# Third batch's second quad: its roots moved amid the GELUs of the second w_in stage, with two more bank pairs for tiles 6 to 9

## The chip, the core and the metric

The kernel runs on one core of a Trainium2 chip. The metric is device time in microseconds (us) of one execution; lower is better. All times below are us unless marked ns. Engines are named as in the profile: PE (matrix multiply), ACT (activations), DVE (vector), POOL, and SP, which only issues DMAs.

## What is computed

Cosine attention over 8 batches, 12 heads, 448 positions and head size 64, followed by a feed-forward block with an exact GELU:

```python
q_n = q / (norm(q) + 1e-6);  k_n = k / (norm(k) + 1e-6)
scores = q_n @ k_n.T / tau
attn = softmax(scores)                 # over the keys
x = (attn @ v), heads joined           # 3584 x 768
out = gelu(x @ w_in) @ w_out           # 768 -> 2048 -> 768
```

Inputs and output are float32; the multiplications take bf16.

## The kernel before

**Work and stages.** Four heads make a *quad* (three to a batch); quads are counted through all batches, so quads 3, 4, 5 belong to the second batch (`b = 1`) and quads 6, 7, 8 to the third. For `b = 0` a stage `attention_first` runs, for the others `attention(b, fill)`; each is followed by `first(b)`, the w_in stage with its GELUs. The output product (w_out, `second_pieces`, line 352) of one batch is cut into single matmuls, `fill`, and these are run in portions (`run()`, line 597) between the attention steps of the next batch. The order of all instructions is written out by hand (`manual_schedule`): each engine executes its own queue in the order in which the program calls for it.

**Preparing a quad.** For each quad: load q and k (`load_qk`, SP, four buffers); square them on POOL (`square`, line 156); add the squares up on DVE (`reduce`, line 165, 2.0 us); take the root as exp(0.5 ln) on ACT (`logs` line 172, `roots` line 181); add 1e-6 on POOL (line 190) and take the reciprocal on DVE (line 192), both in `inverses`; multiply on POOL (`scale`, line 208, two instructions); and transpose by a DMA from SP (`transposes`, line 220). Roots are taken for a *group* of quads at once. These lists use *units*: unit u is quad u - 1, since quad 0 is cut in two. `groups` (line 114) holds lists of units: before, units 7 and 8 (quads 6 and 7) share group 6; units 9 and 10 share group 7. `upto(f, n)` calls f for all items below n that were not called yet, so a call with a small n can do nothing.

**Attention.** A quad has seven chunks of keys. `visit(b, pairs)` takes the next chunks of batch b: for each, scores (PE, line 246) into a pair of PSUM banks, and the exp (ACT, line 253) out of it. There are three pairs, `st0`, `st1` and `st2`. `both(g, p)` finishes quad g: sums of the exps (PE, line 275), `turned` and `inverted` and `spread` on DVE, values (PE, line 289) into bank pair p, and `normalise` (DVE, line 323), which writes x. Sums, output tiles and most tiles of the w_in stage use two more banks in turn, `mm0` and `mm1` (`mm_tile`); a finished output tile is copied out by DVE (line 356) and stored by SP.

**The w_in stage.** `first(b)` makes 16 tiles of 128 columns of x @ w_in, six matmuls each (line 655), and a GELU for each on ACT (line 691). `pairs` (line 650) says which tiles take a pair of banks: `{2: 0, 4: 1}` puts tiles 2 and 3 into `st0`, and 4 and 5 into `st1`; other tiles take `mm0` and `mm1` in turn. The first six tiles are begun with four of their six matmuls, and finished when x is complete. Ln and Exp use another activation table than Gelu, so ACT loads a table when it changes over (lines 647, 693, 695, 700). In batch 0 such a change stands behind tile 5's GELU already: `root(5)` is taken there. In all batches, `first(b)` prepares quads of the next batches: scale and transposes of two quads, a load, squares and sums of two quads.

Of the kernel before, what the change touches and what calls it, by code (L numbers as in the profile page):

```python
# [16 lines left out]
def kernel(  # L17
# [20 lines left out]
    NQ = H // 4  # L38
# [60 lines left out]
    def mm_tile(name, shape=(128, 512), dtype=F32, aside=None):  # L99
        t = ps_mm.tile(list(shape), dtype, tag=f"mm{turn[0] if aside is None else turn[0] ^ aside}", name=name)  # L100
        if aside is None:
            turn[0] ^= 1
        return t

    def pair(i, name):
        pool = third[0] if i == 2 else ps_st
        return pool.tile([128, 2, 512], F32, tag=f"st{i}", name=name)
# [3 lines left out]

    units = [(0, 0, 1), (0, 1, 2)] + [(g, 0, 2) for g in range(1, NG)]
    NU = len(units)
    groups = [[n] for n in range(NQ + 2)] + [[NQ + 2, NQ + 3], [2 * NQ + 1, 2 * NQ + 2]]
    for n in range(3 * NQ, NU, NQ):
        groups += [[n, n + 1], [n + 2]] if n + 2 < NU else [[n]]
    shapes = [[len(gr), 2, units[gr[0]][2] - units[gr[0]][1], C] for gr in groups]
# [51 lines left out]
    def logs(n):  # L169
        nq = nq_t.pop(n)  # L170
        ln_t[n] = nrm.tile(list(nq.shape), F32, tag="lq", name=f"lq{n}")
        nc.scalar.activation(ln_t[n], nq, AF.Ln, bias=tiny)

    def roots(n):
        ln = ln_t.pop(n)
        if n <= NQ:
            sr_t[n] = root2[n % len(root2)][:, :math.prod(shapes[n])]
            nc.scalar.activation(sr_t[n][:, :, 0], ln.rearrange("p j i s c -> p (j i s c)"), AF.Exp, scale=0.5)
        else:
            sr_t[n] = nrm.tile(list(ln.shape), F32, tag="sr", name=f"sr{n}")  # L180
            nc.scalar.activation(sr_t[n], ln, AF.Exp, scale=0.5)  # L181

    def inverses(n):
        sr = sr_t.pop(n)
        shape = [128] + shapes[n]
        se = nrm.tile(shape, F32, tag="se", name=f"se{n}")
        if n <= NQ:
            nc.vector.tensor_reduce(se.rearrange("p j i s c -> p (j i s c)"), sr, mybir.AxisListType.X, ALU.add)
        else:
            nc.gpsimd.tensor_scalar(se, sr, 1e-6, None, ALU.add)  # L190
        rn = nrm.tile(shape, F32, tag="rn", name=f"rn{n}")
        nc.vector.reciprocal(rn, se)  # L192
        rn_t[n] = rn
# [20 lines left out]
    def transposes(u, i=None):  # L214
        g, s0, s1 = units[u]
        qkb = qkb_t[g]
        if g not in qkT_t:
            qkT_t[g] = qkTp.tile([128, 2, C, 128], BF16, tag="qkT", name=f"qkT{g}")
        if i is None:
            nc.sync.dma_start_transpose(out=qkT_t[g].rearrange("p i c s -> p (i c) s"),  # L220
                                        in_=qkb.rearrange("p i c s d -> p (i c s d)"))
            return
        tp = tp_t[u, i] = mm_tile(f"tp{u}_{i}", (128, C, 128), BF16)
        for c in range(C):
            nc.tensor.transpose(tp[64 * s0:64 * s1, c, :], qkb[:, i, c, s0:s1].rearrange("p s d -> p (s d)"), ident)  # L225

    def copies(u, i):
        g, s0, s1 = units[u]
        rows = slice(64 * s0, 64 * s1)
        nc.vector.tensor_copy(qkT_t[g][rows, i], tp_t.pop((u, i))[rows])  # L230
# [94 lines left out]
    def both(g, p):  # L325
        sums(g)
        turned(g)
        inverted(g)
        spread(g, 0)
        spread(g, 1)  # L330
        values(g, p=p)
        normalise(g, 0)
        normalise(g, 1)
# [64 lines left out]
    def upto(f, n, last=None):  # L398
        last = {load_qk: NG, load_v: NV, root: len(groups), load_wi: 4, load_wo: 4}.get(f, NU)
        while done.get(f, 0) < min(n, last):  # L400
            done[f] = done.get(f, 0) + 1
            f(done[f] - 1)
# [180 lines left out]
    def visit(b, pairs):  # L583
        for p in pairs:
            n, c = passes[at.get(b, 0)]
            at[b] = at.get(b, 0) + 1
            scores(b * NQ + n, ((0, c), (1, c)), p)
            exps(b * NQ + n, ((0, c), (1, c)))

    def attention(b, fill):  # L590
        fill = list(fill)
        if len(fill) == 128:
            parts = iter((20, 18, 20, 22, 32, 16))
        else:
            parts = iter((20, 13, 14, 17, 16, 16) if b == 1 else (16, 14, 16, 18, 16, 16))

        def run():
            for _ in range(next(parts)):
                fill.pop(0)()

        x_t[b] = xp.tile([128, KD, S], BF16, tag="x", name=f"x{b}")
        g0, u = b * NQ, b * NQ + 1
        run()
        upto(scale, u + 3)
        upto(transposes, u + 3)
        if b == 1:
            upto(load_qk, g0 + NQ + 2)
            upto(square, u + 4)
        visit(b, (0, 1, 2))
        if b > 1:  # L610
            upto(scale, u + 4)
            upto(transposes, u + 4)
        run()
        visit(b, (0, 1, 2))
        run()
        upto(load_qk, g0 + NQ + 3)
        visit(b, (0, 1) if b <= 2 else (0, 1, 2))
        upto(reduce, u + 4)
        upto(square, u + 5)
        run()  # L620
        visit(b, (0, 1, 2))
        both(g0, 0)
        upto(load_v, b + 3)
        upto(load_qk, g0 + NQ + 4)
        visit(b, (1, 2))
        upto(reduce, u + 5)
        run()
        visit(b, (1, 2, 0))
        both(g0 + 1, 1)
        visit(b, (2, 0))  # L630
        n = 2 * b + 4
        if n < len(groups):
            logs(n)
            roots(n)
        run()
        both(g0 + 2, 2)
        if n < len(groups):
            inverses(n)
            done[root] = n + 1
            if b > 1:  # L640
                visit(b + 1, (0, 1))

    def first(b):
        sb, hf = divmod(b, 2)
        if hf == 0:
            g_t[sb] = gp.tile([128, KF, 2 * S], BF16, tag="g", name=f"g{sb}")
        nc.scalar.preload_act_table_set(GELU_SET)
        u = (b + 1) * NQ + 1
        hps = {}
        pairs = {2: 0, 4: 1} if b else {0: 1, 2: 0, 6: 1, 8: 0}  # L650
        ahead = 6 if b else 5

        def mm(m, kds):
            for kd in kds:
                nc.tensor.matmul(hps[m], lhsT=wi[:, kd, m * 128:(m + 1) * 128],  # L655
                                 rhs=x_t[b][:, kd, :], start=(kd == 0), stop=(kd == KD - 1))

        def bank(m):
            if m in pairs:
                st = pair(pairs[m], f"hp{b}_{m}")  # L660
                hps[m], hps[m + 1] = st[:, 0, :S], st[:, 1, :S]
            elif m not in hps:
                hps[m] = mm_tile(f"hp{b}_{m}")[:, :S]

        for m in range(ahead):
            bank(m)
            mm(m, range(KD - 2))
        if b == 0:
            upto(square, u + 3)
            upto(scale, u + 1)  # L670
            upto(transposes, u + 1)
            upto(load_wo, 4)
            upto(reduce, u + 3)
        else:
            upto(scale, u + 2)
            upto(transposes, u + 2)
            upto(load_qk, (b + 1) * NQ + 5)
            upto(square, u + 4)
            upto(reduce, u + 4)
        for m in range(ahead):  # L680
            mm(m, range(KD - 2, KD))
        for m in range(KF):
            if b == 0 and m == 8:
                for i in range(2):
                    transposes(4, i)
                    copies(4, i)
            if m >= ahead and (m == 0 or m - 1 not in pairs):
                for k in range(m, m + 1 + (m in pairs)):
                    bank(k)
                    mm(k, range(KD))  # L690
            nc.scalar.activation(g_t[sb][:, m, hf * S:(hf + 1) * S], hps.pop(m), AF.Gelu)  # L691
            if b == 0 and m == 5:
                nc.scalar.preload_act_table_set(EXP_SET)
                upto(root, 6)
                nc.scalar.preload_act_table_set(GELU_SET)
                upto(scale, u + 2)
                upto(transposes, u + 2)
                upto(load_qk, 2 * NQ + 1)
        if b + 1 < B:
            nc.scalar.preload_act_table_set(EXP_SET)  # L700
            if b <= 1:
                visit(b + 1, (0, 1, 2))
            upto(root, 2 * b + 6)

    upto(load_qk, 1)
    nc.scalar.preload_act_table_set(EXP_SET)
# [3 lines left out]
    late = nrm.tile([128, 1], F32, tag="late", name="late", bufs=1)  # L710
# [56 lines left out]
```

## Time and profile before

| | us |
|---|---|
| median of 8 runs | 415.7 (415.43 to 417.17) |
| profiled execution, its own time | 415.43 |
| its span, first to last instruction | 413.7 |
| stage `attention(1)` on PE | 53.0 to 80.5 |
| stage `first(1)` on PE | 80.5 to 98.8 |
| stage `attention(2)` on PE | 99.5 to 132.2 |

All times in the text are from the start of the span. A group line of the profile reads: line, engine, operation, output<-input, shapes, count; then busy time and the mean in ns of one; then the idle time of the engine before them and what ended it. Timelines give start and duration. PE's matmuls are pipelined and their ends are modelled: where one follows another at pace, its modelled end lies behind the other's start. The largest groups:

```profile
L253 ACT ACTIVATE pt<-st 128x896 bf16<-128x896 f32 x168 | 142.9, 916 | 66.6 <-PE st L246 66.3
L352 PE MATMUL op<-wo,g 128*128 128x384 bf16 x864 | 147.8, 326 | 0.0
L655 PE MATMUL hp<-x,wi 128*128 128x448 bf16 x768 | 146.8, 353 | 0.0
L691 ACT ACTIVATE g<-hp 128x448 bf16<-128x448 f32 x128 | 65.9, 545 | 70.7 <-PE hp L655 70.5
L208 POOL TENSOR_TENSOR qkb<-qk,rn 128x896 bf16<-128x896 f32 (+1 forms) x49 | 79.6, 1651 | 40.6 <-DVE rn L192 40.6
L165 DVE TENSOR_REDUCE nq<-sq 128x28 f32<-128x1792 f32 (+2 forms) x30 | 48.8, 1637 | 57.6 <-POOL sq L156 54.8
```

### The profile page before, as it was taken

What the parts mean: (1) busy time and instruction counts of PE and PEld (TensorE: products, weight loads), DVE (VectorE), ACT (ScalarE), POOL (GpSimd) and SP (SyncE); (2) the same over time, 40 slices, a digit from 0 to 9 for tenths busy, and PEclk for the clock granted to TensorE, in tenths of its full rate; (3) what the DMA queues carried; (4) which work ended last, traced back from release to release, by engine and by line L of the source; (5) the groups of instructions that cost most, each with busy time, mean ns of one, the idle gap of its engine ahead of it and who ended that gap; (6) DMA issues with size and microseconds to landing.
All of it is one profiled execution on the core that took longest, in us unless ns stands there. A gap on an engine that the chain in (4) does not pass through costs nothing.

```text
span 413.7 us, 8268 instructions
## 1 busy us (share of the span) xinstructions
PE 407.1 (98%) x3506; PEld 212.5 (51%) x3506; DVE 188.4 (46%) x379; ACT 246.3 (60%) x358; POOL 167.0 (40%) x113
## 2 busy tenths in 40 slices
PE   7999999999999999999999999999999999999996
PEld 3444554555555555555555555555555555555564
DVE  4777217913278222943148331783118711481021
ACT  6895686546646567654764658755665467754300
POOL 4999706083810919054730537217370233000000
PEclk9999999999999999999999999999999999999999
DMA  8999998734396505935296332965078120510033
GB/s 289 259 261 207 205 232 279 177 68 112 64 224 200 124 11 91 287 87 122 21 222 207 68 105 46 217 189 133 2 143 218 40 44 2 120 41 0 0 78 77
DMA packets 66996, 54.53 MB, mean 132 GB/s; under 512 B 38672, under 2 KB 62352, under 8 KB 66960
## 3 DMA queue, kind: packets, MB, share of 16 engines
q1 hardware_dynamic: 54464, 41.79, 39.2%
q0 software_dynamic: 12112, 11.80, 18.0%
q8 instruction: 27, 0.44, 0.4%
q10 hardware_dynamic: 384, 0.43, 0.3%
q14 instruction: 9, 0.07, 0.1%
HBM read 45.61 MB, written 11.01 MB: 137 GB/s over the span
## 4 chain that ended last, share of the span: by engine, by line
PE 94%; DMA 2%; ACT 1%; DVE 1%; POOL 1%; issue 0%; SPq 0%; POOLq 0%
PE hp L655 35%; PE op L352 32%; PE st L246 9%; PE o L289 8%; PE sm L275 4%; PE spin L407 2%; DMA qk<-in_k_dram 2%; PE op L371 1%; PE sm L266 1%; PE tp L225 1%; ACT pt L253 1%; POOL sq L156 1%; DVE nq L165 0%; DVE qkT L230 0%; ACT g L691 0%
## 5 line engine op out<-in xcount | busy, mean ns | idle before, releaser
L253 ACT ACTIVATE pt<-st 128x896 bf16<-128x896 f32 x168 | 142.9, 916 | 66.6 <-PE st L246 66.3
L352 PE MATMUL op<-wo,g 128*128 128x384 bf16 x864 | 147.8, 326 | 0.0
L655 PE MATMUL hp<-x,wi 128*128 128x448 bf16 x768 | 146.8, 353 | 0.0
L352 PEld LDWEIGHTS <-g 128*128 128x128 bf16 x864 | 81.5, 98 | 62.3 <-issue 10.9
L655 PEld LDWEIGHTS <-wi 128*128 128x128 bf16 x768 | 74.4, 98 | 71.4 <-issue 2.9
L691 ACT ACTIVATE g<-hp 128x448 bf16<-128x448 f32 x128 | 65.9, 545 | 70.7 <-PE hp L655 70.5
L208 POOL TENSOR_TENSOR qkb<-qk,rn 128x896 bf16<-128x896 f32 (+1 forms) x49 | 79.6, 1651 | 40.6 <-DVE rn L192 40.6
L165 DVE TENSOR_REDUCE nq<-sq 128x28 f32<-128x1792 f32 (+2 forms) x30 | 48.8, 1637 | 57.6 <-POOL sq L156 54.8
L356 DVE COPY ot<-op 128x384 f32<-128x384 f32 x54 | 29.5, 548 | 95.5 <-PE op L352 93.4
L156 POOL TENSOR_TENSOR sq<-qk 128x1792 f32<-128x1792 f32 (+1 forms) x22 | 66.5, 3037 | 12.8 <-DMA qk<-in_k_dram 12.8
L190 POOL TENSOR_SCALAR se<-sr 128x28 f32<-128x28 f32 (+1 forms) x14 | 4.4, 312 | 125.4 <-ACT sr L181 125.3
L246 PE MATMUL st<-qkT 64*64 64x448 bf16 x672 | 47.7, 358 | 0.2
L289 PE MATMUL o<-pt,v 64*64 64x448 bf16 x672 | 36.9, 352 | 0.0
L246 PEld LDWEIGHTS <-qkT 64*64 64x64 bf16 x672 | 18.3, 105 | 23.8 <-issue 15.4
L318 DVE STREAM_TRANSPOSE rs<-rc 128x448 f32<-128x448 f32 x48 | 28.1, 623 | 0.8
L323 DVE TENSOR_TENSOR x<-o,rs 128x448 bf16<-128x448 f32 x48 | 27.0, 599 | 1.0 <-DVE rs L318 0.5
L192 DVE RECIPROCAL rn<-se 128x28 f32<-128x28 f32 (+2 forms) x18 | 6.8, 376 | 43.4 <-POOL se L190 43.2
L289 PEld LDWEIGHTS <-v 64*64 64x64 bf16 x672 | 17.7, 106 | 16.9 <-issue 8.4
L297 DVE STREAM_TRANSPOSE tr<-sm 128x448 f32<-128x448 f32 x24 | 15.5, 647 | 13.8 <-PE sm L275 10.7
L275 PE MATMUL sm<-pt,ones 128*32 128x448 bf16 (+1 forms) x336 | 17.8, 332 | 0.3 <-DVE ot L356 0.3
L309 DVE TENSOR_REDUCE tr<-tr 32x28 f32<-32x28 f32 x84 | 16.4, 196 | 1.6
L407 PE MATMUL spin<-blank,ident 128*128 128x448 bf16 x34 | 10.5, 458 | 2.2 <-DVE root L89 1.9
(43 smaller groups left out, 115.8 us busy)
## 6 DMA issues: line engine op xcount, KB each, us to landing
qk<-in_q_dram SPq DMA_DIRECT2D x23, 448.0 KB, 6.6
qk<-in_k_dram SPq DMA_DIRECT2D x23, 448.0 KB, 8.6
out_dram<-ot SPq DMA_DIRECT2D x48, 192.0 KB, 3.4
v<-in_v_dram POOLq DMA_DIRECT2D x7, 672.0 KB, 11.7
wi<-in_moe_w_in_dram POOLq DMA_DIRECT2D x8, 384.0 KB, 13.1
wo<-in_moe_w_out_dram POOLq DMA_DIRECT2D x4, 768.0 KB, 13.3
out_dram<-ot SPq DMA_DIRECT2D x12, 96.0 KB, 2.2
qk<-in_q_dram SPq DMA_DIRECT2D x2, 224.0 KB, 3.5
```

Of the source, the lines that this page charges most:

```text
L156: eng.tensor_tensor(sq[:, part], t[:, part], t[:, part], ALU.mult)
L165: nc.vector.tensor_reduce(nq[:, part], sq[:, part], mybir.AxisListType.X, ALU.add)
L208: eng.tensor_tensor(qkb[:, i, :, s0:s1].rearrange("p c s d -> p s c d"), t[:, i, s0:s1], rn[:, i].to_broadcast([128, s1 - s0, C, D]), ALU. ...
L246: nc.tensor.matmul(st[cols, n, :S], lhsT=qkT[rows, 1, c, cols], rhs=qkT[rows, 0, :, cols], start=True, stop=True, tile_position=(64 * s, 6 ...
L253: nc.scalar.activation(pt[:, :m], st[:, :m, :S], AF.Exp, scale=inv_tau)
L275: nc.tensor.matmul(bank_t[g, "sm"][r:r + 32, cols], lhsT=ones, rhs=pt_t[g, s, c][:, cols], start=(c < 2), stop=(c >= C - 2), tile_position ...
L289: nc.tensor.matmul(bank_t[g, h][cols, :S], lhsT=v_t[g][rows, s, c, :], rhs=pt_t[g, s, c][rows], start=(c == 0), stop=(c == C - 1), tile_po ...
L318: nc.vector.transpose(rs, bank_t[g, "rc"][:, h].to_broadcast([128, NB, 32]))
L352: nc.tensor.matmul(ps[:, :NH], lhsT=g_t[sb][:, kf, t * 128:(t + 1) * 128], rhs=wo[:, kf, ni * NH:(ni + 1) * NH], start=(kf == 0), stop=(kf ...
L356: nc.vector.tensor_copy(ot[:, ni * NH:(ni + 1) * NH], ps[:, :NH])
L655: nc.tensor.matmul(hps[m], lhsT=wi[:, kd, m * 128:(m + 1) * 128], rhs=x_t[b][:, kd, :], start=(kd == 0), stop=(kd == KD - 1))
L691: nc.scalar.activation(g_t[sb][:, m, hf * S:(hf + 1) * S], hps.pop(m), AF.Gelu)
```

## The change

Group 6 is cut in two: unit 7 (quad 6) and unit 8 (quad 7) get a group each, and the numbers of all later groups go up by one; most edits only follow that numbering. What is done at another place or in another way:

- `attention(1)`: quad 6's sum of squares moves from ahead of the fourth `run()` portion to behind `both(g0, 0)`, that is behind quad 3's `normalise`. Quad 7's sum, which stood there, moves into `first(1)`. The roots near the end of `attention(1)` are those of quad 6 alone.
- `first(1)`: the stage begins with scale and transposing DMA of quad 6 alone, the load of quad 10, the square of quad 8, and the sum of quad 7. Behind tile 5's GELU come a table load, Ln and Exp of quad 7, a table load, and then quad 7's `inverses`, scale and transposing DMA, the square of quad 9, and the sums of quads 8 and 9. Tiles 6 and 7 take pair `st2`, tiles 8 and 9 pair `st0`; they took `mm0` and `mm1` in turn.
- From batch 2 on, the calls of `reduce` that are left out did nothing, as the sums had been made in `first`.

```diff
--- before.py
+++ after.py
@@ -111,7 +111,7 @@
 
     units = [(0, 0, 1), (0, 1, 2)] + [(g, 0, 2) for g in range(1, NG)]
     NU = len(units)
-    groups = [[n] for n in range(NQ + 2)] + [[NQ + 2, NQ + 3], [2 * NQ + 1, 2 * NQ + 2]]
+    groups = [[n] for n in range(NQ + 2)] + [[NQ + 2, NQ + 3], [2 * NQ + 1], [2 * NQ + 2]]
     for n in range(3 * NQ, NU, NQ):
         groups += [[n, n + 1], [n + 2]] if n + 2 < NU else [[n]]
     shapes = [[len(gr), 2, units[gr[0]][2] - units[gr[0]][1], C] for gr in groups]
@@ -615,7 +615,6 @@
         run()
         upto(load_qk, g0 + NQ + 3)
         visit(b, (0, 1) if b <= 2 else (0, 1, 2))
-        upto(reduce, u + 4)
         upto(square, u + 5)
         run()
         visit(b, (0, 1, 2))
@@ -623,12 +622,12 @@
         upto(load_v, b + 3)
         upto(load_qk, g0 + NQ + 4)
         visit(b, (1, 2))
-        upto(reduce, u + 5)
+        upto(reduce, u + 4 + (b > 1))
         run()
         visit(b, (1, 2, 0))
         both(g0 + 1, 1)
         visit(b, (2, 0))
-        n = 2 * b + 4
+        n = 2 * b + 4 + (b > 1)
         if n < len(groups):
             logs(n)
             roots(n)
@@ -647,7 +646,7 @@
         nc.scalar.preload_act_table_set(GELU_SET)
         u = (b + 1) * NQ + 1
         hps = {}
-        pairs = {2: 0, 4: 1} if b else {0: 1, 2: 0, 6: 1, 8: 0}
+        pairs = ({0: 1, 2: 0, 6: 1, 8: 0}, {2: 0, 4: 1, 6: 2, 8: 0}, {2: 0, 4: 1})[min(b, 2)]
         ahead = 6 if b else 5
 
         def mm(m, kds):
@@ -672,11 +671,12 @@
             upto(load_wo, 4)
             upto(reduce, u + 3)
         else:
-            upto(scale, u + 2)
-            upto(transposes, u + 2)
+            late = int(b == 1)
+            upto(scale, u + 2 - late)
+            upto(transposes, u + 2 - late)
             upto(load_qk, (b + 1) * NQ + 5)
-            upto(square, u + 4)
-            upto(reduce, u + 4)
+            upto(square, u + 4 - late)
+            upto(reduce, u + 4 - 2 * late)
         for m in range(ahead):
             mm(m, range(KD - 2, KD))
         for m in range(KF):
@@ -689,18 +689,22 @@
                     bank(k)
                     mm(k, range(KD))
             nc.scalar.activation(g_t[sb][:, m, hf * S:(hf + 1) * S], hps.pop(m), AF.Gelu)
-            if b == 0 and m == 5:
+            if b <= 1 and m == 5:
                 nc.scalar.preload_act_table_set(EXP_SET)
-                upto(root, 6)
+                upto(root, 6 if b == 0 else 8)
                 nc.scalar.preload_act_table_set(GELU_SET)
                 upto(scale, u + 2)
                 upto(transposes, u + 2)
-                upto(load_qk, 2 * NQ + 1)
+                if b == 0:
+                    upto(load_qk, 2 * NQ + 1)
+                else:
+                    upto(square, u + 4)
+                    upto(reduce, u + 4)
         if b + 1 < B:
             nc.scalar.preload_act_table_set(EXP_SET)
             if b <= 1:
                 visit(b + 1, (0, 1, 2))
-            upto(root, 2 * b + 6)
+            upto(root, 2 * b + 6 + (b > 0))
 
     upto(load_qk, 1)
     nc.scalar.preload_act_table_set(EXP_SET)
```

## Prediction

> **What bounds the kernel now.** I read the page first, then TensorE's waits, then the chain, then the timelines around each edit.
>
> ```profile
> span 413.7 us, 8268 instructions
> PE 407.1 (98%) x3506; PEld 212.5 (51%) x3506; DVE 188.4 (46%) x379; ACT 246.3 (60%) x358; POOL 167.0 (40%) x113
> PEclk9999999999999999999999999999999999999999
> PE 94%; DMA 2%; ACT 1%; DVE 1%; POOL 1%; issue 0%; SPq 0%; POOLq 0%
> ```
>
> PE is busy in 98% of the span at a full clock, and 94% of the chain is PE. A busy PE need not be at its peak, so I looked for pace: stage 2 of batch 1 has 96 matmuls from 80.53, busy 18.33; less one modelled length (0.35) that is 17.98 for 95 steps, 0.189 each, with no hole. Who made PE wait is a list of three lines:
>
> ```profile
> PE spin L407 <- DVE root L89: 1.9, 1, 1.9
> PE spin L407 <- DVE qkT L230: 0.3, 1, 0.3
> PE sm L275 <- DVE ot L356: 0.3, 1, 0.3
> ```
>
> (line, releaser: total us, times, longest.) The first two lie in the opening stage, which the change does not touch. The third is the only hole that PE shows behind 33 us, and the chain, in order of time, leaves PE just there:
>
> ```profile
> 53.08 7.94 DMA qk<-in_k_dram
> 61.14 3.19 POOL sq L156
> 64.35 2.02 DVE nq L165
> 66.89 0.85 PE sm L275 x16
> ```
>
> So the kernel is PE-bound, and an edit off PE can save no more than this one hole; it can lose more, by making PE wait.
>
> **The hole, and what the change removes.** DVE's and PE's timelines there (start, us, what; idle before and releaser in brackets):
>
> ```profile
> 64.35 2.02 DVE L165 TENSOR_REDUCE nq<-sq 128x28 f32<-128x1792 f32 x1 [4.43 <-POOL sq L156]
> 66.29 1.01 DVE L356 COPY ot<-op 128x384 f32<-128x384 f32 x2
> ```
>
> ```profile
> 65.86 0.76 PE L246 MATMUL st<-qkT 64*64 64x448 bf16 x12
> 66.89 0.85 PE L275 MATMUL sm<-pt,ones 128*32 128x448 bf16 x16 [0.27 <-DVE ot L356]
> ```
>
> DVE stands still for 4.43 us in front of quad 6's sum of squares (third batch, quad 0), because POOL's square of it is late; behind it wait two copies of finished output tiles. The first of these tiles was done at about 63.3; `sums` of quad 3 takes that tile's bank, so PE waits for the copy. Scores ended at 65.86 + 0.76 = 66.62 and sums began at 66.89: 0.27 idle. Without a wait the modelled ends overlap: one quad later scores at 72.20 last 0.76 and sums begin at 72.89, 0.07 before their end. The hole is worth 0.27 + 0.07 = **0.34 us**. The change puts this sum of squares behind quad 3's `normalise`, where quad 7's stood (72.07, 2.00 us). There DVE has as much work as before; the square has long been done; the copies run at about 63.4 and 66.0, and the hole goes.
>
> **What is late next.** PE comes 0.34 earlier, but the exps of the scores at 65.86 do not: ACT has three, 66.30 to 68.83. `values` of quad 3 (67.66, now 67.32) needs the first pair free; its exp ends at 66.30 + 0.92 = 67.22, and a release took 0.04 (66.85 to 66.89): no wait. The second scores pair behind (69.20, now 68.86) needs the third exp's bank: 68.83 + 0.04 to 0.06, a wait of about 0.02. One quad later the same sequence runs without the hole (72.20 to 75.02), and there only one wait of 0.06 can be read; so I take 0.02, bounds 0 and 0.10.
>
> **What it adds: a detour on ACT.** Amid batch 1's GELUs, behind tile 5's, come a table load, a Ln, an Exp and a table load, with ten GELUs queued behind them and PE waiting for banks behind those. Before has the same detour in batch 0:
>
> ```profile
> 38.04 2.81 ACT L691 ACTIVATE g<-hp 128x448 bf16<-128x448 f32 x6 [4.06 <-PE hp L655]
> 40.87 1.28 ACT L693 ACT_TABLE_LOAD   x1
> 42.34 0.34 ACT L172 ACTIVATE lq<-nq,tiny 128x56 f32<-128x56 f32 x1 [0.19 <-DVE nq L165]
> 42.72 0.25 ACT L181 ACTIVATE sr<-lq 128x56 f32<-128x56 f32 x1
> 42.98 1.28 ACT L695 ACT_TABLE_LOAD   x1
> 44.28 0.98 ACT L691 ACTIVATE g<-hp 128x448 bf16<-128x448 f32 x2
> ```
>
> From the end of the sixth GELU (40.85) to the next (44.28) it takes 3.43, of which 0.19 is a wait for DVE. Half as wide (28 columns) Ln and Exp save 0.05 together: 3.43 - 0.19 - 0.05 = 3.19. In batch 1 GELU 5 ends at 87.66 + 0.99 = 88.65 (times before the shift by the hole, which moves ACT and PE alike), so GELU 6 starts at 91.84 instead of 88.68. GELUs that stand ready follow each other by 0.98 - 0.545 = 0.435 (two take 0.98, one 0.545): GELU 10 starts at 93.58 and ends at 94.13 to 94.16.
>
> This is why tiles 6 to 9 get two pairs: PE runs through them, and tiles 10 and 11 find banks of GELUs 0 and 1. The first PE instruction that needs a GELU behind the detour is tile 12's first, for tile 10's bank. By PE's pace it is due at 80.53 + 72 x 0.1893 = 94.16; the bank is released at 94.17 to 94.20. **Wait: 0.03 us.** Bounds: nothing, or, if the five GELUs don't overlap at all, 91.84 + 5 x 0.545 + 0.04 - 94.16 = 0.45. I take 0.03, because the paced rows stand in this same stage. Tile 13 needs GELU 11, which starts with its own tile's end: caught up. The pair of tiles 6 and 7 was last read by quad 5's normalise, which tile 0's fifth matmul (85.1) waits for anyway.
>
> A rule speaks against this edit. The Trainium skill ("ScalarE: Activation LUTs", What ACT_TABLE_LOAD costs, and the rule to batch calls by set) puts a switch of sets at 1283 ns and a drain of about 1380 ns. The load agrees with the row (1283 in all 16 of lines 647, 693 and 700); the drain would show as idle time behind a load, and the rows above have 0.02, 0.19 and 0.02. By the page the detour would be an estimated 2 x 2.66 + 0.55 = 5.87, tile 12's wait 2.7, and the time 418.1.
>
> **What it moves, costed at nothing, with the cover.**
> - Root of quad 6 alone at 77.10: Ln and Exp narrower by 0.05; ACT then idles 6.63 before GELU 0.
> - Sum of squares of quad 7, now behind the reciprocal at 83.48 (0.48, narrower now): done at about 85.9; Ln wants it at 88.65 + 1.30 = 89.95. Cover 4 us; DVE stood idle there for 9.95 us.
> - POOL does quad 6's scale, then quad 8's square, then a new `se` (0.31) that waits for the Exp (90.5), then quad 7's scale and quad 9's square: 90.5 + 0.31, reciprocal 0.4, scale 3.33, square 3.17, sum 2.02 = 99.8 instead of 99.06. The Ln that reads it starts at 103.16. Cover 3.3 us; without it the exps behind that Ln, then the scores at 106.68, come late by as much.
> - SP: quad 7's transposing DMA goes from 90.77 to about 94.8 and lands 4.0 later, at 98.8. Quad 6's seven chunks are read at 98.79 (three), 102.84 (three) and 106.68, so quad 7's scores come at 106.9; cover 8 us, and the slowest one in the trace (issued at 53.73, landed 10.2 us later) would still do. Quad 10's load, issued ahead of it, goes from 92.36 to about 89; it is squared behind 111 us.
> - SP again: the store of the early copy no longer blocks its queue from 63.3 to 67.3, so quad 9's load (68.56) moves up some 3 us, into the loads of quads 7 and 8. These may land later; quad 7's square (66.64) feeds a sum that is now wanted at 83.9.
> - PE's instructions, 7,014 with the weight loads, come in the same order in both programs. Behind batch 1 the other engines do the same work under group numbers raised by one.
>
> **Sum.** -0.34 + 0.02 + 0.03 = -0.29 us. The profiled execution took 415.43 (span 413.7 and 1.7 around it): 415.14. The median of the eight runs is 415.7, 0.27 higher, so I predict **415.4**. Bounds of the parts: -0.34 to -0.24 + 0.45 = +0.21, so 415.4 to 415.9.
>
> **Rivals.** 0.2% is 0.83 us, about what a measurement of this kernel can tell from no change.
> 1. The gain is eaten: tile 12's wait is near its upper bound, or another wait takes the place of the copy's (the second copy, the exps). 415.6 to 416.1. For: the margins are 0.02 to 0.06 us. Against: the same sequence one quad later, and the paced GELUs. Chance 0.22.
> 2. Slower: the detour is long because its Ln waits for quad 7's sum, which stands on DVE behind a reciprocal that waits for POOL, and ten GELUs wait in order behind it. The batch 0 row has such a wait (0.19). From 89.95 on each us goes to tile 12; with the hole's gain it shows from a sum that ends at about 91. Were it done at 92, the wait is 2.05 + 0.03: 415.4 + 2.05 = 417.4. Against: 4 us of cover. With all else that makes PE wait, 0.12.
> 3. Faster by over 0.83: no hole behind 33 us is that large; only drift of the measurement or a loss that PE's records hide. Under 414.9. Chance 0.05.
>
> Forecast 0.61. Within 0.2%: 0.61 + 0.22 = 0.83; slower 0.12; faster 0.05. The range takes the bounds 415.4 to 415.9, the medians' scatter (six of the eight runs lie within 0.3) and the near part of rival 2: 414.9 to 416.5.
>
> **What would show it.** Right: no wait of sums L275 for a copy; the 2.0 us sum behind quad 3's normalise alone; GELU 6 3.2 us behind GELU 5; at tile 12 a step of PE of under 0.25 instead of 0.19; the stage behind starting 0.3 earlier. Wrong: idle time before the Ln or between the loads, a tile 12 step of over 0.6, a Ln at 103 that waits, or scores at 107 that wait for a transpose.

## The result, and the profile after

The changed kernel takes 414.79 us (median of 24 runs, 414.52 to 415.57); the kernel before, run beside it, 415.99 (67 runs, 415.26 to 419.55). The ratio is 0.9968, 95% interval 0.9959 to 0.9977: faster by 0.3%, some 1.2 to 1.3 us, four times what was forecast, and just below the stated range. The profiled execution took 414.62 (span 412.8), against 415.43 (413.7).

The page of the changed kernel:

```profile
span 412.8 us, 8274 instructions
PE 405.9 (98%) x3506; PEld 212.0 (51%) x3506; DVE 188.6 (46%) x380; ACT 248.8 (60%) x362; POOL 167.3 (41%) x114
PE 85%; POOL 8%; DMA 4%; DVE 1%; issue 1%; ACT 0%; POOLq 0%
```

Whom PE waited for in it (us in total, times, longest):

```profile
PE spin L407 <- DVE root L89: 1.9, 1, 1.9
PE tp L225 <- DVE qkb L208: 0.4, 1, 0.4
PE tp L225 <- POOL qkb L208: 0.4, 2, 0.2
PE st L246 <- DVE qkT L230: 0.2, 1, 0.2
PE st L246 <- DMA qkT<-qkb: 0.2, 1, 0.2
```

The wait of the sums for a copy is gone. DVE's and then PE's timeline of the changed kernel at that place:

```profile
62.73 0.56 DVE L356 COPY ot<-op 128x384 f32<-128x384 f32 x1 [3.83 <-PE op L352]
65.33 0.56 DVE L356 COPY ot<-op 128x384 f32<-128x384 f32 x1 [2.04 <-PE op L352]
66.82 0.65 DVE L297 STREAM_TRANSPOSE tr<-sm 128x448 f32<-128x448 f32 x1 [0.93 <-PE sm L275]
```

```profile
65.23 0.76 PE L246 MATMUL st<-qkT 64*64 64x448 bf16 x12
65.92 0.85 PE L275 MATMUL sm<-pt,ones 128*32 128x448 bf16 x16
```

The copies run as soon as their tiles are done, and sums follow scores at pace. But PE was early before it came here: the two profiles differ already in the opening. PE's first lines of the kernel before, then of the changed one:

```profile
1.93 6.88 PE L407 MATMUL spin<-blank,ident 128*128 128x448 bf16 x20 [1.93 <-DVE root L89]
8.86 0.94 PE L225 MATMUL tp<-ident,qkb 128*64 128x128 bf16 x14
10.65 0.38 PE L246 MATMUL st<-qkT 64*64 64x448 bf16 x2
```

```profile
1.93 5.24 PE L407 MATMUL spin<-blank,ident 128*128 128x448 bf16 x20 [1.93 <-DVE root L89]
7.57 0.58 PE L225 MATMUL tp<-ident,qkb 128*64 128x128 bf16 x7 [0.40 <-DVE qkb L208]
9.65 0.94 PE L246 MATMUL st<-qkT 64*64 64x448 bf16 x8 [0.22 <-DVE qkT L230]
```

The 20 filler matmuls took 6.88 and 5.24: PE goes at one per 0.37 first and at one per 0.19 later, and the change came at 7.86 in the one and at 4.50 in the other. PE's first scores start 1.01 earlier. Matmul by matmul, the changed kernel's PE stands 1.01 ahead from there; 0.63 behind the wait at 58.97 (for a transposed quad, which lands at 58.93); 0.97 behind the sums at 65.92 (0.34, the hole); 0.93 behind the scores that follow (0.04 lost); 0.85 behind tile 12 (0.08 lost), and so to the end. So in this pair of profiles the edit itself gave 0.34 - 0.04 - 0.08 = 0.22 us; the rest is the opening.

So the profiles offered two readings. **Theory A**: the hole is *pinned*. It ends when quad 6's load, square and sum are done, whatever PE did before; its size is that moment less PE's arrival. The profile of before happened to have a slow opening, so PE came late and the hole was small. In other executions the hole is 1.3 us, and what PE wins in the opening is lost there. **Theory B**: the opening is faster in the changed program by itself, and the hole is 0.34. **Theory C**: the detour or the bank pairs bring the gain.

### The profile page after: what moved, and what is told of

Its sections match the earlier page's. It is cut to its first block, busy times and chain, and to the rows that moved or that the text cites. A ratio compares the mean times of both kernels' runs of the same rounds, so it can differ in the third digit from the quotient of the medians.

```text
span 412.8 us, 8274 instructions
## 1 busy us (share of the span) xinstructions
PE 405.9 (98%) x3506; PEld 212.0 (51%) x3506; DVE 188.6 (46%) x380; ACT 248.8 (60%) x362; POOL 167.3 (41%) x114
## 4 chain that ended last, share of the span: by engine, by line
PE 85%; POOL 8%; DMA 4%; DVE 1%; issue 1%; ACT 0%; POOLq 0%
PE op L352 34%; PE hp L654 31%; PE st L246 8%; PE o L289 7%; PE sm L275 4%; POOL qkb L208 4%; DMA qkT<-qkb 3%; POOL sq L156 2%; PE op L371 1%; POOL wi L385 1%; DMA qk<-in_q_dram 1%; DVE nq L165 1%; POOL wo L392 0%; POOL v L141 0%; DVE rn L192 0%
## 5 line engine op out<-in xcount | busy, mean ns | idle before, releaser
L275 PEld LDWEIGHTS <-ones 128*32 128x32 bf16 x336 | 6.8, 96 | 9.0 <-issue 7.2
```

What stands on the lines that cost most here:

```text
L275: nc.tensor.matmul(bank_t[g, "sm"][r:r + 32, cols], lhsT=ones, rhs=pt_t[g, s, c][:, cols], start=(c < 2), stop=(c >= C - 2), tile_position ...
```

## Experiments

Every time is a median; "beside it" is the kernel before, run alongside.

**The kernel before, once more**, without an edit.

> The kernel before, unchanged, looked at once more. Theory A (the hole in front of quad 3's sums is pinned: it ends when the third batch's first load, square and sum of squares are done, at about 66.9 to 67.2 us whatever PE did, so its size is that moment less PE's arrival): in this profile sums of quad 3 start at 66.8 to 67.3 again, whether the opening is slow (first scores at 10.65) or fast (9.65), and a fast opening shows a hole of 0.9 to 1.4 us instead of 0.34. Theory B (the changed kernel's opening is faster by itself, and the hole is 0.34 us): this profile shows the slow opening again, first scores at about 10.65, and a hole of 0.3 to 0.4.

415.66, beside it 416.00; ratio 0.9991 (0.9973 to 1.0009). Its opening was fast. Its waits, and its chain where it leaves PE (start, us, what):

```profile
PE sm L275 <- DVE ot L356: 1.3, 1, 1.3
```

```profile
51.89 9.22 DMA qk<-in_k_dram
...
61.24 3.18 POOL sq L156
...
64.45 2.02 DVE nq L165
66.47 0.48 DVE ot L356
66.94 0.04 issue
66.98 0.85 PE sm L275 x16
```

PE's first scores started at 9.68, 0.97 earlier than in the first profile of the same kernel, and sums at 66.98, 0.10 *later*. Its span is 413.8 against 413.7. The load was issued 1.2 earlier (51.34 against 52.52, q part) and its k part landed at 61.12 against 61.02: an earlier PE does not bring it earlier. A holds, and B is out: the fast opening belongs to no program.

The traces of all runs show what the load follows. In the 13 that leave it in its place, its k part landed 2.44 to 2.46 behind quad 4's transposed tile, whose DMA SP issues ahead of it, although it was issued anywhere from 51.67 to 53.29. That tile landed between 58.30 and 58.93 in twelve of them and at 59.87 in one, while PE's first scores came anywhere from 9.65 to 11.41. So the moment is pinned by that transfer; it is not the same in every execution.

**The sum alone.** No detour, no further pairs; quad 7's sum is left out.

```diff
-        upto(reduce, u + 4)
+        if b > 1:
+            upto(reduce, u + 4)
...
-        upto(reduce, u + 5)
+        if b == 1:
+            upto(reduce, u + 4)
+            nc.vector.tensor_copy(nq_t[6][:, 1], nq_t[6][:, 0])
+            done[reduce] = u + 5
+        else:
+            upto(reduce, u + 5)
```

> The kernel before with quad 6's sum of squares behind quad 3's normalise, and no detour, no extra bank pairs. Quad 7's sum of squares is left out (a small copy of quad 6's takes its place, so quad 7 is scaled with quad 6's roots). Theory A: the whole gain is here, 1.1 to 1.5 us under the kernel before, ratio 0.9964 to 0.9974. Theory B (hole of 0.34, and a faster opening that belongs to the changed program): 0.3 to 0.4 us under it, ratio about 0.999. Theory C (the detour or the bank pairs bring the gain in some later stage): within 0.4 us of the kernel before.

414.91, beside it 416.00; ratio 0.9967 (0.9950 to 0.9984), the changed kernel's 0.9968. As far as the intervals tell, all the gain is in the moved sum, as A had it; C is out. (That it isn't the missing sum of quad 7: the next run keeps this sum where the changed kernel has it.) Its waits have no line of sums, only the opening's:

```profile
PE spin L407 <- DVE root L89: 1.9, 1, 1.9
PE spin L407 <- DVE qkT L230: 0.2, 1, 0.2
```

**The detour alone.** The changed kernel with the sum back at its old place.

```diff
         visit(b, (0, 1) if b <= 2 else (0, 1, 2))
+        if b == 1:
+            upto(reduce, u + 4)
         upto(square, u + 5)
```

> The changed kernel with quad 6's sum of squares back ahead of the fourth portion of output matmuls; detour, bank pairs and numbering of groups stay. Theory A: the hole is back, sums of quad 3 start at 66.8 to 67.3, and the time is that of the kernel before plus tile 12's wait, ratio 1.000 to 1.0004. Theory B: 0.7 to 0.9 us under the kernel before. Theory C: 1 us under it.

415.95, beside it 416.00; ratio 0.9994 (0.9975 to 1.0012): no gain. First scores at 9.79, sums at 67.15, and the hole is back:

```profile
PE sm L275 <- DVE ot L356: 1.2, 1, 1.2
```

**No further pairs.** The changed kernel with `{2: 0, 4: 1}` for batch 1.

> The changed kernel with tiles 6 to 9 of batch 1 in the two single banks in turn. The detour ends as in the changed kernel, some 3.2 us behind the sixth GELU; the first matmul that needs a GELU behind it is now tile 8's. By the changed kernel's times (last six GELUs end at 87.7, seventh from 90.97 to 91.51; tile 8 due at about 88.7) PE waits 2.8 to 2.9 us there, and the time is 2.7 to 3.0 us over the changed kernel, about 1.5 over the kernel before. If the detour did not decide PE's wait, the time would stay within 0.3 us of the changed kernel.

418.93, beside it 416.00; ratio 1.0069 (1.0044 to 1.0094). The wait is there and of the size expected (tile 8 starts 2.88 later than at pace), but the time is 4.1 over the changed kernel, not 2.7 to 3.0. PE's timeline, and a table of windows whose last three columns are granted clock, DMA share and GB/s:

```profile
85.75 2.81 PE L654 MATMUL hp<-x,wi 128*128 128x448 bf16 x14
91.28 4.95 PE L654 MATMUL hp<-x,wi 128*128 128x448 bf16 x17 [2.72 <-ACT g L691]
```

```profile
80.00:88.40 8.40, 8.40 (x46) 4.30 (x44) 4.42 (x7) 3.79 (x7) 5.68 (x3) 1.00 0.24 55
91.20:94.50 3.30, 3.23 (x9) 1.28 (x9) 0.77 (x1) 1.00 (x3) 3.30 (x3) 0.50 0.49 182
94.60:98.00 3.40, 3.40 (x20) 1.76 (x19) 1.32 (x1) 1.50 (x3) 2.04 (x1) 1.00 0.73 135
```

Nine matmuls fill 3.3 us behind the wait, where 17 or 18 would at pace: the granted clock is 0.50, and comes back at about 94.5. That is another 1.6. With the wait's 2.88 it makes 4.5, by which this span (416.9) exceeds that of the sum alone (412.4), where PE's first scores came at 9.73 as they did here. The Trainium skill ("TensorE: Matmul & The Clock Gate", What's actually happening) says that an idle window of some 3.4 us halves PE's clock and a busy one restores it; here 2.7 of idle time were enough. So the pairs are what makes the detour nearly free, and a wait of PE that is long enough costs more than its length.

**The square twice**, in both kernels: POOL 3.17 later ahead of quad 6's sum.

```diff
+            square(u + 3)
             upto(square, u + 4)
```

> The kernel before with POOL squaring quad 6 twice in a row, 3.17 us more ahead of its sum of squares. Theory A (that sum's end decides when quad 3's sums start): the whole 3.2 us are added to the hole, which reaches 4.5 us in a run with a fast opening (3.5 with a slow one); time at least 3.0 us over the kernel before, and up to 1.4 more if PE runs its next matmuls at half pace behind so long a hole, as it did behind the 2.9 us wait of the kernel without the extra pairs. Theory B (a hole of 0.34 that is no more than a DVE queue of copies): about 3 us too, so this run tells A and B apart only together with the changed kernel's twin.

> The changed kernel with POOL squaring quad 6 twice in a row. Theory A: quad 6's sum now stands behind quad 3's normalise at 71.1 us and the square ends at about 67.8, so nothing waits: time within 0.3 us of the changed kernel. If POOL's lateness still reached PE by another way (quad 7's square, the v load behind it on POOL's queue), 1 us or more would be added.

The kernel before takes 421.12 (beside it 415.80; ratio 1.0119, 1.0098 to 1.0139), 5.3 more. Its DVE and PE lines:

```profile
68.90 2.02 DVE L165 TENSOR_REDUCE nq<-sq 128x28 f32<-128x1792 f32 x1 [9.05 <-POOL sq L156]
70.84 1.01 DVE L356 COPY ot<-op 128x384 f32<-128x384 f32 x2
```

```profile
66.17 0.76 PE L246 MATMUL st<-qkT 64*64 64x448 bf16 x12
71.44 1.13 PE L275 MATMUL sm<-pt,ones 128*32 128x448 bf16 x12 [4.51 <-DVE ot L356]
```

The hole is 4.5. The opening was a slow one here (first scores at 10.59), for which 3.5 was expected: the other 1.0 comes from quad 6's load, which landed at 62.32, 1.3 later than in the first profile (PE too came 0.3 later). PE's next stretch at half pace added 2.2, more than the 1.4 allowed. This execution (422.19) is one of the two longest of six; the others lie between 420.59 and 421.14. The changed kernel takes 414.77 (beside it 415.80; 0.9976, 0.9958 to 0.9995): its median has nothing added, though one of its 12 runs took 418.71. The same 3.17 on POOL cost 5.3 in the one and nothing in the other. That is the edit's work.

**Eight more filler matmuls** in both kernels: PE late in the opening.

```diff
-    spin(20)
+    spin(28)
```

> The kernel before with 28 filler matmuls ahead of the opening instead of 20: PE's first scores come 0.8 to 1.5 us later. Theory A: the hole takes it up (1.3 us with a fast opening, 0.3 with a slow one): the median moves by 0 to 0.5 us, and the sums of quad 3 start at 66.8 to 67.3 again unless PE itself is later than that. Theory B: the full 0.8 to 1.5 us are added to the time.

> The changed kernel with 28 filler matmuls ahead of the opening instead of 20. Theory A: there is no hole to take it up, so the time grows by 0.5 to 1.3 us (the first 0.2 to 0.4 may be taken up by PE's wait for a transposed quad at 58.9), and the two kernels come closer: less than 0.7 us between the medians of this one and of the kernel before with 28. Theory B: both grow by the same and stay 1.2 us apart.

Before: 416.29, beside it 415.80, ratio 1.0001 (0.9989 to 1.0013). Changed: 415.72, which is 0.93 over its 414.79; ratio 0.9984 (0.9963 to 1.0006). They are 0.57 apart instead of 1.2. The medians are as A expects, but the two intervals overlap, so this pair alone does not rule B out. The profile of the first is a weak test too: PE's pace doubled early in it (at 4.86), so that the first scores came at 10.65 in spite of the eight matmuls, just as in the first profile of all. Its hole is larger than there by 0.3, the time by which quad 6's load landed later (61.34 against 61.02):

```profile
PE sm L275 <- DVE ot L356: 0.6, 1, 0.6
```

In the changed kernel PE's first scores came at 11.41, 0.76 later than in the first profile of before, and 0.54 of that is still there at the end: no hole takes it up, and the 0.22 that is gone is what the edit gave in the first pair of profiles.

**The load first.** The kernel before, with the head of the pinned chain moved instead of its end.

```diff
+                upto(load_qk, 2 * NQ + 1)
                 upto(scale, u + 2)
                 upto(transposes, u + 2)
-                upto(load_qk, 2 * NQ + 1)
```

> The kernel before, with quad 6's load issued ahead of the transposing DMA of quad 4 that its queue holds it behind (issued at 47.4, blocking SP for 5.0 us); the sums stay where they were. Theory A traces the pinned end of the hole back to this load (issued at 52.5 and 53.1, landed at 61.0, then 3.2 for the square and 2.0 for the sum): landed 2 us or more earlier, the hole is gone, and the time is 1.0 to 1.4 us under the kernel before although no sum was moved, unless quad 4's transposed tile, which PE reads at 58.7, now lands later; each us by which it does is a new wait of PE there. If the hole stays with the load landed before 59, theory A has the wrong head of the chain.

418.61, beside it 415.58; ratio 1.0073 (1.0046 to 1.0099): slower, by the proviso and not by the main clause. Quad 6's square now starts at 50.12, its sum at 59.34: the load does set when they come, as A has it. But quad 4's transposed tile lands at 61.84 instead of 58.66, and PE comes to quad 3's sums only at 70.21. The sums follow the scores at pace (0.28 from start to start), but so late a PE would have met no hole with the old load either; A's time without the hole was not put to the test. PE's timeline:

```profile
58.92 0.38 PE L246 MATMUL st<-qkT 64*64 64x448 bf16 x4
61.88 0.96 PE L246 MATMUL st<-qkT 64*64 64x448 bf16 x8 [2.58 <-DMA qkT<-qkb]
62.77 3.44 PE L352 MATMUL op<-wo,g 128*128 128x384 bf16 x14
```

2.6 of idle time; the output matmuls behind it follow each other first at 0.30 to 0.32 (six steps), then at 0.16. All 12 runs are slower (416.74 to 421.72).

**Two attempts at more.** Tiles 10 and 11 of batch 1 in the third pair (`10: 1` added to `pairs`), 16 filler matmuls instead of 20, and both.

> The changed kernel with tiles 10 and 11 of batch 1 in the third bank pair as well (its last tiles 4 and 5 were read long before). The first matmul that needs a GELU behind the detour is then tile 14's, 2.3 us later, so the step of 0.27 us at tile 12 becomes 0.19: 0.08 us under the changed kernel in the trace, which the times can't tell from no change. If something other than the late GELUs made that step, it stays.

> The changed kernel with 16 filler matmuls ahead of the opening instead of 20. Nothing behind takes an opening's lateness up any more, so in executions where the filler ends late (8.86 us in the first profile of the kernel before, by the page the data for the first transposes being there at about 7.6 to 7.9) 4 x 0.19 = 0.75 us are saved, in the others nothing: median 0.1 to 0.4 us under the changed kernel, and no run near 415.6. If PE, left idle before the first transposes, falls back to half pace, it loses 0.5 us or more instead.

> Both edits: 0.1 to 0.5 us under the changed kernel, about 414.3 to 414.7 where that has 414.8.

415.00, 414.61 and 414.47, beside them 415.62; ratios 0.9975 (0.9959 to 0.9992), 0.9975 (0.9961 to 0.9990) and 0.9969 (0.9954 to 0.9984). The step at tile 12 is gone with the fifth pair: no step of the stage is over 0.2. None can be told from the changed kernel by its time. The shorter filler missed its expectation: 5 of its 12 runs still lie between 415.1 and 415.8.

## Why the prediction was wrong

- **What bounds the kernel**: right. PE's order is the same in both, and the only wait behind 33 us was the one removed.
- **"The hole is worth 0.34 us"**: this term failed. I read the hole as a property of the kernel; it was one execution's difference of two moments. With the other opening it was worth 1.33 (a step of 1.61 instead of 0.28), and taking it away alone brought the whole gain (ratio 0.9967). Two executions with an opening alike, the kernel before once more (415.52) and the sum alone (414.22), lie 1.30 apart; the changed kernel's (414.62) lost 0.38 at 58.97 and 0.08 at tile 12 as well. The row at hand was right: in that execution the hole gave 0.34, and matmul by matmul the changed kernel gained 0.34 there, 0.22 of which its other terms left, where the sum had 0.29. What I didn't ask is whether the two moments move together. The chain that I quoted, DMA, POOL, DVE, PE, said that they don't: the hole's end was set by a load that was issued at 53, before PE did the 13 us of work that led up to the hole.
- **"The first two lie in the opening, which the change does not touch"**: true and beside the point. The change removes what *absorbed* the opening's spread. Before, a fast or a slow opening gave spans of 413.8 and 413.7; now it goes through to the end, but for the wait at 58.97.
- **The spread**: I took the runs' scatter for noise around a median. The profiled 415.43 was among the lowest of before, and 16 of its 67 runs lie above 416.5, none of the changed kernel's 24. That a late load makes that tail is argued, not shown: one profile, that of the doubled square in the kernel before, has a load 1.3 late and a hole 1.0 larger than expected, but no profile of the kernel as it was fell into the tail.
- **"No hole behind 33 us is that large"**, the argument against rival 3, fell with the hole's term: rival 3's time (under 414.9) is what came, through a hole larger than the profile showed.
- **The exps**: PE lost 0.04 at the scores behind, forecast 0.02, within the bounds of 0 and 0.10.
- **The detour**: 3.19 forecast from GELU 5's end to GELU 6, 3.26 measured. ACT's timeline of the changed kernel:

```profile
86.73 0.99 ACT L691 ACTIVATE g<-hp 128x448 bf16<-128x448 f32 x2
87.73 1.28 ACT L693 ACT_TABLE_LOAD   x1
89.03 0.32 ACT L172 ACTIVATE lq<-nq,tiny 128x28 f32<-128x28 f32 x1
89.43 0.23 ACT L181 ACTIVATE sr<-lq 128x28 f32<-128x28 f32 x1
89.68 1.28 ACT L695 ACT_TABLE_LOAD   x1
90.97 2.29 ACT L691 ACTIVATE g<-hp 128x448 bf16<-128x448 f32 x5
```

  The Exp starts 0.08 behind the Ln's end instead of 0.03. Behind the loads stand 0.02 and 0.01: the drain of about 1.38 a switch, which the Trainium skill adds ("ScalarE: Activation LUTs", What ACT_TABLE_LOAD costs), does not show here either. Tile 12 waited 0.08 (a step of 0.27 instead of 0.19), forecast 0.03, bound 0.45: the mechanism and the place were right, and the fifth pair removed it.
- **The covers** held. The slowest transposing DMA of the trace was mis-read: the one issued at 47.39 took 11.2, not 10.2, and would still have done. Quad 7's sum was done at 84.7, its Ln started at 89.03; the last sum ended at 98.99, its Ln started at 102.31; quad 7's transposed tile landed at 97.81. The store was mis-read: it waits for the second of the two copies (65.33), so quad 9's load moved up by 1.4 and not by 3. PE's instructions with the weight loads are 7,012 on the page (3506 and 3506), not 7,014.

## What to carry to other kernels

A wait in one profile is the difference of two moments. Follow both back: if the releaser's chain goes through a load and PE's through earlier PE work, the wait can be larger in other executions, and it swallows whatever PE gains or loses ahead of it; what removing it is worth has to be bounded by the spread of PE's arrival too. A spread of runs that is lopsided, with the profiled one near the bottom, may be a hint of such a place. And a change that moves a load can pay for it on another transfer: removing the consumer's wait was worth 1.1 us, bringing the load forward cost 3.0.

## What the runs showed of the hardware

- The moment when PE's pace doubles in the opening differs between executions: 4.50 to 7.86 us in the twelve profiles with 20 or 28 filler matmuls, with PE busy from 1.93 in all. The windows of the profile give a granted clock of 1.00 for that time too, but its records begin only with the doubling (at 7.91 in before, at 5.02 in before once more); the pace tells it. The Trainium skill ("TensorE: Matmul & The Clock Gate", What's actually happening) explains it by a free-running window of 3.41 us. The spread found here, 3.4, is of that size, and wider than the 0.5 to either side that the same section names.
- 2.6 to 2.7 us of idle time were enough to halve PE's clock: six steps of output matmuls at 0.30 to 0.32 instead of 0.16 (load first), nine w_in matmuls in 3.3 us (no pairs). A wait of 1.3 did not.
- The transposing DMA of quad 4 landed 0.1 to 1.0 behind the second w_out load, which was issued 6 us before it, in all 14 profiles: 58.56 and 57.80 (before), 58.66 and 58.11 (before, once more), 58.93 and 58.33 (changed), 59.87 and 59.26 (before, square twice), 61.84 and 61.76 (load first). That it waits for that load was not tried.
